# Squares one step later, feed-forward steps dealt by due time, and decay transfers of 104 rows, in a fused RWKV-7 and squared-ReLU kernel

## The chip, the core and the metric

The kernel runs on one core of a Trainium2 chip. Its engines take their instructions in order, each from its own queue, and wait for one another through semaphores: TensorE (PE in the profile, with its weight loads PEld), VectorE (DVE), ScalarE (ACT), GpSimd (POOL) and SyncE (SP), which here only issues DMAs. The metric is the device time of one execution in microseconds (us), taken as the median over several runs.

## What is computed

An attention block (a recurrence over 768 positions, 4 batches, 8 heads of dimension 40) and then a feed-forward block on its output:

```python
for t in range(S):                       # 768 positions, state is D x D per batch and head
    y[:, :, t] = einsum('bhd,bhde->bhe', r_t, state)
    Sa = einsum('bhde,bhe->bhd', state, a_t)
    state = state * w_t - outer(Sa, b_t) + outer(v_t, k_t)
x = y.transpose(0, 2, 1, 3).reshape(B * S, H * D)      # 3072 x 320
out = (maximum(x @ w_in, 0) ** 2) @ w_out              # w_in 320 x 2048, w_out 2048 x 320
```

## The kernel before, in words

**Attention.** The sequence is cut into six chunks of 128 positions, so with four batches there are 24 blocks, called slots here and counted by `i` in `order`. For each slot there are three generators. `early(i)` (L338) turns the decays and the inputs a and b, makes running products of the decays (two scans per pair of heads, L348 and L349, and two reciprocals, L352 and L353), multiplies them into a and b (L356, L357), and stores the result, a tile `decay` of 128 partitions by 1,560 floats, in the DRAM tile `kept_e` (L359). Two heads lie in one tile at partitions 0 and 64, each 40 rows high, so rows 0 to 103 hold data and the rest is padding. `rest(i)` (L491) prepares what can be made before the state is known: it turns k (L501), multiplies it by the decays to `kvT` (L503), multiplies that with a in TensorE (`masked("A", ...)`, L509), turns r and v (L513, L515), makes `RV` (L525), and scales k and b (L535). `chain(i)` (L558) does what needs the state, in up to eleven steps: the products with the state, the solve with two half inverses (`times_t`, L587), the new state (L617), `RX` (L621), and the output `tokens` (L636). `solve` (L411) makes the inverses on GpSimd.

**Decays.** For slots 0 and 1 `early` writes the decays straight into a tile `dec`, taken from a pool of two buffers (L341). From slot 2 on, `load(i)` (L148) takes a `dec` from the same two buffers and loads it from `kept_e`. There are 22 stores and 22 loads, all from SP's queue.

**Feed-forward.** Three slots make a group of 384 tokens (`GB = 3`). When the last slot of a group has its `tokens`, eight small DMAs (L641) move parts of them to other partitions, and two ticks later the group counts as gathered (L642). The generator `ffn()` (L648) then works through the group in 28 steps. Sixteen steps go up: matmuls with `w_third` (for two steps at a time) and `w_in` into PSUM, then a ReLU on ScalarE (L663), then the square of the same tile on VectorE (L664). Twelve steps go down: four matmuls with `w_out` each; every fourth copies its result (L677) and stores 128 tokens (L679). Eight groups are 224 steps in all. A step that is asked for while no group is gathered does nothing (`yield False`).

**The order of the work** is written out by the program itself: the loop at L786 runs `weave` (L691) once per slot, with twelve places per slot. In each place the generators are advanced in a fixed order: `chain(i)`, then the feed-forward, then `early` of a later slot, then `rest(i + 1)`. Each spreads its steps evenly: ten feed-forward steps over twelve places leave places 0 and 6 without one. All engines' queues follow this order. `share` (L782) gives no feed-forward steps to slots 0 to 3, eight to slot 4, and ten to each slot from 5 on; what is left runs after the loop (L812).

The line numbers of the profile are those of the code below.

Of the kernel before, what the change touches and what calls it, by code (L numbers as in the profile page):

```python
# [8 lines left out]
FP32 = mybir.dt.float32  # L9
I32 = mybir.dt.int32  # L10
U32 = mybir.dt.uint32
Alu = mybir.AluOpType
# [5 lines left out]
def kernel(  # L18
# [22 lines left out]
    nc = tc.nc  # L41
    ctx.enter_context(tc.manual_schedule())
    B, H, S, D = r.shape
    DM = H * D
    DFF = moe_w_in.shape[1]
    C = 128
# [3 lines left out]
    NP = H // 2  # L50
    DP = 64
    NF = DFF // 128
    GB = 3
# [7 lines left out]
    for h, d, n in ((6, 0, D), (7, 0, D), (5, HALF, D - HALF)):  # L61
        while n:
# [5 lines left out]
            d, n = d + m_, n - m_  # L68
# [8 lines left out]
    dram = ctx.enter_context(tc.tile_pool(name="dram", bufs=1, space=bass.MemoryType.DRAM))  # L77
# [4 lines left out]
    def psum(pool):  # L82
        name = "ps_" + pool.name[-1]
        return pool.tile([128, 512], FP32, tag=name, name=name)
# [4 lines left out]
    def single(name, shape):  # L89
        return const.tile(shape, FP32, tag=name, name=name)  # L90

    def new(name, shape, bufs):
        return work.tile(shape, FP32, tag=name, name=name, bufs=bufs)
# [4 lines left out]
    def later(fn, steps=2):  # L98
        line.append([steps, fn])
# [7 lines left out]
    def store(out_, in_, steps=2, queue=nc.sync):  # L107
        later(lambda: queue.dma_start(out=out_, in_=in_), steps)  # L108
# [27 lines left out]
    order = [(bb, c) for c in range(NCH) for bb in range(B)]  # L136
# [11 lines left out]
    def load(i, g=None):  # L148
        x_ = loaded[i] = {"k": fetch("k", k, i)}
        if g is not None:  # L150
            g["dec"] = new("dec", [128, 3, NP, C + 2], 2)
            nc.sync.dma_start(out=g["dec"], in_=kept_e[i])
        x_["r"] = fetch("r", r, i)
        later(lambda: x_.update(v=fetch("v", v, i), b=fetch("b", b, i)), 2 if g is not None else 0)

# [22 lines left out]

    UP, DOWN, A_ = range(3)
    decays = Ring("decay", 2, [128, 3, NP, C + 2], 1.0, whole)  # L180
    minus_x = Ring("minus_x", 1, [128, H, DP], 0.0, pads)
    states = Ring("state", B, [128, NP, 2, DP], 0.0, whole)

# [92 lines left out]
    def as_they_are():  # L276
# [4 lines left out]
        for f in range(NF):  # L281
# [6 lines left out]

    kept_n = [dram.tile([HC, H, HC], FP32, tag=f"n{i}", name=f"kept_n{i}") for i in range(len(order))]
    Q = HC // 2  # L290
    kept_e = [dram.tile([128, 3, NP, C + 2], FP32, tag=f"e{i}", name=f"kept_e{i}") for i in range(len(order))]

    sizes = [1, 1] + [2] * 4 + [4] * ((len(order) - 12) // 4) + [2]
    units = [(sum(sizes[:u]), n) for u, n in enumerate(sizes)]
# [11 lines left out]
                        tag=f"t{u}", name=f"kept_t{u}") for u, (_, nb) in enumerate(units)]  # L306
# [31 lines left out]
    def early(i, g=None):  # L338

        x_ = early_loaded.pop(i)  # L340
        dec = decays.next() if g is None else new("dec", [128, 3, NP, C + 2], 2)  # L341
        if g is not None:
            nc.vector.memset(dec[:, :A_, :, MID:MID + 1], 1.0)
        up, down, aT = (dec[:, n] for n in (UP, DOWN, A_))
        wT = turn(x_["w"])
        yield
        for q in range(NP):
            nc.vector.tensor_tensor_scan(up[:, q, MID + 1:C + 1], wT[:, q, MID:], ones, 1.0, Alu.mult, Alu.mult)  # L348
            nc.vector.tensor_tensor_scan(down[:, q, MID - 1::-1], wT[:, q, MID - 1::-1], ones, 1.0, Alu.mult, Alu.mult)  # L349
        yield  # L350
        bT_, aT_ = turn(x_["b"]), turn(x_["a"])
        nc.vector.reciprocal(down[:, :, MID + 1:C + 1], up[:, :, MID + 1:C + 1])  # L352
        nc.vector.reciprocal(up[:, :, :MID], down[:, :, :MID])  # L353
        yield
        bT = turned("bT", 1)
        nc.vector.tensor_tensor(bT, bT_, down[:, :, 1:C + 1], Alu.mult)  # L356
        nc.vector.tensor_tensor(aT[:, :, :C], aT_, up[:, :, :C], Alu.mult)  # L357
        if g is None:
            store(kept_e[i], dec)  # L359
        yield  # L360
        bb, c = order[i]
        t_ = new("N", [128, H, C], 1)
        even, odd = products(bT, aT[:, :, :C])
        nc.scalar.copy(t_[:, :NP], even)

        for half in range(2):
            own_, other = (slice(n * HC, (n + 1) * HC) for n in (half, 1 - half))
            nc.scalar.copy(t_[own_, NP:, own_], odd[other, :, other])
        nc.scalar.copy(t_[:HC, NP:, HC:], odd[:HC, :, HC:])
        joins = lambda half: t_[half * HC:half * HC + Q, :, half * HC + Q:(half + 1) * HC]  # L370
        for half in range(2):
            for n in range(2):
                at = half * HC + n * Q
                if i < SMALL:
                    kept, to = kept_q[i, :, half, n], at + Q
                else:
                    u = unit_of[i]
                    kept, to = kept_d[u][i - units[u][0], :, half], (half + 1) * HC
                    kept = kept[:, n * Q * HC:n * Q * HC + Q * (to - at)].rearrange("h (s t) -> h s t", s=Q)
                store(kept.rearrange("h s t -> s h t"), t_[at:at + Q, :, at:to], 1, nc.scalar if g is not None and n else nc.sync)  # L380
            if i < SMALL and g is None:
                store(kept_m[i][half], joins(half), 1)
        if g is None:
            store(kept_n[i], t_[:HC, :, HC:], 1)
        else:
            g["dec"], g["N"] = dec, new("N21", [HC, H, HC], 2)
            nc.scalar.copy(g["N"], t_[:HC, :, HC:])
            g["joins"] = spare("joins", i)
            for half in range(2):
                nc.scalar.copy(g["joins"][half * HC:half * HC + Q], joins(half))  # L390
        yield
# [253 lines left out]

    PART = NF // 4

    def ffn():  # L648
        for gi in range(len(order) // GB):
            while gi not in gathered or finished[0] < NARROW:  # L650
                yield False
            t_ = tokens.pop(gi)
            hid = []
            for f in range(0, NF, 2):
                ps = [psum(ps_f if gi < len(order) // GB - 1 else ps_w)[:, :GB * C] for _ in range(2)]
                for e, p_ in enumerate(ps):
                    half = slice(e * DP, (e + 1) * DP)
                    mm(p_, w_third[half, f * 64:f * 64 + 128], t_[half, NT, :], True)
                for e, p_ in enumerate(ps):
                    for j in range(NT):  # L660
                        mm(p_, w_in[:, j, (f + e) * 128:(f + e + 1) * 128], t_[:, j, :], False)
                    h_ = hidden[:, f + e]
                    nc.scalar.activation(h_, p_, Act.Relu)  # L663
                    nc.vector.tensor_tensor(h_, h_, h_, Alu.mult)  # L664
                    hid.append(h_)
                    yield True
            while left():
                yield False
            for n in range(GB):
                bb, c = order[gi * GB + n]  # L670
                p_ = psum(ps_f if gi < len(order) // GB - 1 else ps_w)[:, :DM]
                for f in range(NF):
                    mm(p_, hid[f][:, n * C:(n + 1) * C], w_out[:, f], f == 0)
                    if f % PART == PART - 1 and f < NF - 1:
                        yield True
                o_ = new("o", [128, DM], 2)
                nc.scalar.copy(o_, p_)  # L677
                at = bb * S + c * C
                store(out[at:at + C, :], o_)  # L679
                yield True  # L680
# [98 lines left out]
    TOTAL = 12  # L779
    ahead = {0: (4, 5), 1: (6, 7), 2: (8,), 3: (9,), 4: (10, 11), 5: (12, 13)}  # L780
    ahead.update({i: (i + 8,) for i in range(6, len(order) - 8)})
    share = {**{i: (0, 0) for i in range(B)}, B: (8, 4)}  # L782
    pieces_in = {0: (4, TOTAL), 1: (6, TOTAL), 2: (6, TOTAL), 3: (7, TOTAL), B: (4, 4)}
    done = set(range(B))
    unit = unit_of[B]
    for i in range(len(order)):  # L786
        bb, c = order[i]
        n, begin = share.get(i, (10, 0))
        tc.no_sync_barrier()
        g = ready.pop(i)  # L790
        jobs = [(chain(i, g), 11, 0, TOTAL) if i else (first_slot, 10, 0, TOTAL)]
        jobs.append((some(second, n), n, begin, TOTAL))
        made = ahead.get(i, ())
        for j, m_ in enumerate(made):
            jobs.append((prepare(m_), 5, j * 5, TOTAL - 5 * (len(made) - 1 - j)))
        done.update(made)
        if i + 1 < len(order):
            if i:
                ready[i + 1] = {}
                load(i + 1, ready[i + 1])  # L800
            jobs.append((rest(i + 1, ready[i + 1]), 9, 2, TOTAL))
        if i in pieces_in:
            m_, end = pieces_in[i]
            jobs.append((some(rounded, 2 * m_), 2 * m_, 0, end))
        weave(*jobs)
        while unit < len(units) and all(m_ in done for m_ in range(len(order)) if unit_of[m_] == unit):
            flush()
            take(unit, own)
            solve(unit)
            unit += 1  # L810
# [32 lines left out]
```

## Time and profile before

| | |
|---|---|
| median of 6 runs | 1062.65 us (1055.06 to 1066.15) |
| the profiled execution | 1062.29 us, of which the span is 1060.6 us |
| mean granted TensorE clock | 0.903 |
| VectorE, ScalarE, GpSimd busy | 500.1, 272.2, 667.2 us |
| squares L664, 128 of them | 92.7 us, 724 ns each in the mean, 488 to 1623 ns |
| reciprocals L352 | 1740 ns each; scans L348, 267 ns each |
| `kept_e<-decay` and `dec<-kept_e` | 22 each, 780 KB each, issued by SP |
| all DMA traffic | 113.51 MB |
| first feed-forward matmul | 238.6 us |

The span is the time from the first to the last instruction of the execution. "Busy" is the time in which an engine had an instruction in work. The granted clock is the share of full speed that TensorE was given; it changes within a run. In the rows of a window, the columns are: the window, its length, busy time (and number of instructions) of PE, PEld, DVE, ACT and POOL, the granted clock, the DMA engines' mean share, and GB/s. In the rows of a timeline: start, duration, engine, line, operation, output and inputs, form, number of instructions, and in brackets the idle time of the engine before it with what ended it.

### The profile page before, as it was taken

What the parts mean: (1) busy time and instruction counts of PE and PEld (TensorE: products, weight loads), DVE (VectorE), ACT (ScalarE), POOL (GpSimd) and SP (SyncE); (2) the same over time, 40 slices, a digit from 0 to 9 for tenths busy, and PEclk for the clock granted to TensorE, in tenths of its full rate; (3) what the DMA queues carried; (4) which work ended last, traced back from release to release, by engine and by line L of the source; (5) the groups of instructions that cost most, each with busy time, mean ns of one, the idle gap of its engine ahead of it and who ended that gap; (6) DMA issues with size and microseconds to landing.
All of it is one profiled execution on the core that took longest, in us unless ns stands there. A gap on an engine that the chain in (4) does not pass through costs nothing.

```text
span 1060.6 us, 19794 instructions
## 1 busy us (share of the span) xinstructions
PE 942.7 (89%) x7824; PEld 680.5 (64%) x7824; DVE 500.1 (47%) x940; ACT 272.2 (26%) x627; POOL 667.2 (63%) x1124
## 2 busy tenths in 40 slices
PE   6374658769999999999999999999999999999898
PEld 5264556656667766776677667766776577667556
DVE  5465786786463465543662564274324322331120
ACT  3132332442322223113312322123212211231120
POOL 4788465885887699971999943999958960000000
PEclk8666566578889999999999999999999999999899
DMA  8978988857728627348627519504354342220000
GB/s 109 163 141 162 190 223 156 193 132 158 135 60 172 160 25 147 90 89 184 133 33 151 120 72 182 129 34 87 62 136 82 61 97 70 57 37 7 22 1 19
DMA packets 261356, 113.51 MB, mean 107 GB/s; under 512 B 243792, under 2 KB 249424, under 8 KB 259600
## 3 DMA queue, kind: packets, MB, share of 16 engines
q1 hardware_dynamic: 256928, 93.24, 44.5%
q0 software_dynamic: 3248, 18.88, 7.4%
q8 instruction: 62, 1.02, 0.4%
q10 hardware_dynamic: 1088, 0.13, 0.1%
q14 instruction: 30, 0.25, 0.1%
HBM read 75.77 MB, written 34.48 MB: 104 GB/s over the span
## 4 chain that ended last, share of the span: by engine, by line
PE 75%; DVE 7%; DMA 7%; issue 3%; ACT 3%; POOL 3%; SPq 2%; DVEq 0%; ACTq 0%; POOLq 0%
PE ps_f L87 38%; PE ps_c L87 15%; PE ps_w L87 15%; PE ps_w L311 4%; DMA dec<-kept_e 2%; DMA w_out<-in_moe_w_in_dram 1%; SPq L108 1%; POOL half_t L434 1%; POOL half_p L432 1%; DVE decay L352 1%; PE ps_c L577 1%; DMA kept_e<-decay 1%; DVE kvT L503 1%; PE ps_c L541 1%; PE ps_w L531 1%
## 5 line engine op out<-in xcount | busy, mean ns | idle before, releaser
L432 POOL TENSOR_TENSOR half_p<-half_n,half_t 128x70 f32<-128x70 f32 (+52 forms) x502 | 297.5, 593 | 101.2 <-DMA half_n<-kept_d 51.1
L434 POOL TENSOR_TENSOR half_t<-half_t,half_p 128x70 f32<-128x70 f32 (+52 forms) x502 | 322.3, 642 | 39.3
L664 DVE TENSOR_TENSOR hid<-hid 128x384 f32<-128x384 f32 x128 | 92.7, 724 | 245.4 <-ACT hid L663 244.9
L87 PE MATMUL ps_f<-w_out,hid 128*128 128x320 f32 x672 | 200.4, 441 | 0.0
L87 PE MATMUL ps_f<-tokens,w_in 128*128 128x384 f32 x448 | 180.5, 527 | 0.0
L87 PEld LDWEIGHTS ps_f<-w_out,hid 128*128 128x128 f32 x672 | 120.9, 190 | 45.6 <-issue 2.9
L663 ACT ACTIVATE hid<-ps_f 128x384 f32<-128x384 f32 x112 | 54.9, 490 | 265.9 <-PE ps_f L87 265.9
L87 PEld LDWEIGHTS ps_f<-tokens,w_in 128*128 128x128 f32 x448 | 78.9, 196 | 66.3 <-issue 36.3
L87 PE MATMUL ps_f<-tokens,w_third 64*128 64x384 f32 x224 | 55.5, 537 | 2.8 <-DVE w_out L261 2.8
L87 PE MATMUL ps_w<-decay,bT 40*128 40x128 f32 x352 | 29.9, 316 | 30.1 <-DVE decay L357 30.1
L327 DVE TENSOR_TENSOR A<-ps_w,upper 128x512 f32<-128x512 f32 x48 | 30.9, 685 | 45.3 <-PE ps_w L87 45.3
L87 PEld LDWEIGHTS ps_w<-decay,bT 40*128 40x128 f32 x352 | 25.3, 216 | 39.0 <-DVE decay L357 22.6
L348 DVE TENSOR_TENSOR_SCAN decay<-ps_w,ones 128x64 f32<-128x64 f32 x88 | 23.5, 267 | 51.4 <-PE ps_w L311 51.3
L327 DVE TENSOR_TENSOR RX<-ps_w,upper 128x512 f32<-128x512 f32 x48 | 30.8, 683 | 34.3 <-PE ps_w L87 34.1
L87 PE MATMUL ps_w<-dec,kvT 40*128 40x128 f32 x384 | 32.1, 312 | 16.5 <-DVE kvT L503 16.5
L503 DVE TENSOR_TENSOR kvT<-ps_w,dec 128x512 f32<-128x512 f32 x24 | 16.4, 684 | 54.9 <-PE ps_w L311 37.4
L87 PEld LDWEIGHTS ps_w<-dec,kvT 40*128 40x128 f32 x384 | 27.1, 212 | 21.8 <-DVE kvT L503 19.3
L327 DVE TENSOR_TENSOR RV<-ps_w,upper 128x512 f32<-128x512 f32 x48 | 30.9, 685 | 16.3 <-PE ps_w L87 15.8
L352 DVE RECIPROCAL decay<-decay 128x256 f32<-128x256 f32 x22 | 38.3, 1740 | 0.0
L87 PEld LDWEIGHTS ps_c<-xr,T 64*64 64x64 f32 x768 | 29.1, 146 | 14.0 <-issue 10.4
L87 PEld LDWEIGHTS ps_w<-rT,kvT 40*128 40x128 f32 x384 | 27.7, 204 | 15.9 <-DVE RX L327 7.4
L87 PE MATMUL ps_w<-rT,xnT 40*128 40x128 f32 x384 | 34.4, 289 | 3.5 <-ACT rT L513 2.6
(139 smaller groups left out, 1422.2 us busy)
## 6 DMA issues: line engine op xcount, KB each, us to landing
kept_e<-decay SPq DMA_DIRECT2D x22, 780.0 KB
dec<-kept_e SPq DMA_DIRECT2D x22, 780.0 KB
hid<-in_moe_w_out_dram SPq DMA_DIRECT2D x16, 320.0 KB
half_n<-kept_d POOLq DMA_DIRECT2D x12, 384.0 KB, 8.6
half_n<-kept_d POOLq DMA_DIRECT2D x6, 768.0 KB, 10.4
in_w<-in_w_dram SPq DMA_DIRECT2D x24, 160.0 KB
in_ab<-in_b_dram SPq DMA_DIRECT2D x24, 160.0 KB
in_ab<-in_a_dram SPq DMA_DIRECT2D x24, 160.0 KB
```

The costliest lines, as they stand in the source:

```text
L87: nc.tensor.matmul(o, l_, r_, start=start, stop=True, skip_group_check=True)
L108: later(lambda: queue.dma_start(out=out_, in_=in_), steps)
L311: nc.tensor.transpose(p_[:, q * 128:(q + 1) * 128], pair(x_, q), ident)
L327: nc.vector.tensor_tensor(t_, p_, over4(upper), Alu.mult)
L348: nc.vector.tensor_tensor_scan(up[:, q, MID + 1:C + 1], wT[:, q, MID:], ones, 1.0, Alu.mult, Alu.mult)
L352: nc.vector.reciprocal(down[:, :, MID + 1:C + 1], up[:, :, MID + 1:C + 1])
L432: nc.gpsimd.tensor_tensor(p_, part[:, at:at + m_].unsqueeze(1).to_broadcast([128, n, m_]), t3[:, :n, s:s + 1].to_broadcast([128, n, m_]), ...
L434: nc.gpsimd.tensor_tensor(t3[:, :n, s + 1:], t3[:, :n, s + 1:], p_, Alu.subtract)
L503: nc.vector.tensor_tensor(kT, kT_, down[:, :, 1:C + 1], Alu.mult)
L531: nc.tensor.transpose(p_[:, q * 128:(q + 1) * 128], down[:, q, 1:C + 1], ident)
L663: nc.scalar.activation(h_, p_, Act.Relu)
L664: nc.vector.tensor_tensor(h_, h_, h_, Alu.mult)
```

## The change

There are three parts. In the feed-forward, the square of a tile is issued in the following step, after that step's ReLU; the last one is issued at the beginning of the first step down. The steps are dealt by a list `by_then` of how many are to be issued by the end of each slot: at most ten more than the slot before, and from slot 9 on no more than leaves `LAG = 4` of a group for after the slot in which the next group is gathered. The decays' DRAM tiles have 104 rows (`USED = DP + D`), the transfers move these rows only, and the two `dec` buffers are named tiles, `kept_here`, in place of tiles of the pool.

```diff
@@ def load
-            g["dec"] = new("dec", [128, 3, NP, C + 2], 2)
-            nc.sync.dma_start(out=g["dec"], in_=kept_e[i])
+            g["dec"] = kept_here[i % 2]
+            nc.sync.dma_start(out=g["dec"][:USED], in_=kept_e[i])
@@ beside the rings
+    USED = DP + D
+    kept_here = [single(f"dec{n}", [128, 3, NP, C + 2]) for n in range(2)]
@@
-    kept_e = [dram.tile([128, 3, NP, C + 2], FP32, tag=f"e{i}", name=f"kept_e{i}") for i in range(len(order))]
+    kept_e = [dram.tile([USED, 3, NP, C + 2], FP32, tag=f"e{i}", name=f"kept_e{i}") for i in range(len(order))]
@@ def early
-        dec = decays.next() if g is None else new("dec", [128, 3, NP, C + 2], 2)
+        dec = decays.next() if g is None else kept_here[i]
...
-            store(kept_e[i], dec)
+            store(kept_e[i], dec[:USED])
@@ def ffn
+    square = lambda h_: nc.vector.tensor_tensor(h_, h_, h_, Alu.mult)
...
                     nc.scalar.activation(h_, p_, Act.Relu)
-                    nc.vector.tensor_tensor(h_, h_, h_, Alu.mult)
+                    if hid:
+                        square(hid[-1])
                     hid.append(h_)
                     yield True
+            square(hid[-1])
             while left():
@@ before the loop over slots
-    share = {**{i: (0, 0) for i in range(B)}, B: (8, 4)}
+    PER, LAG = NF + 4 * GB, 4
+    by_then = [0] * B + [8]
+    for i in range(B + 1, len(order)):
+        by_then.append(min(by_then[-1] + 10, PER * (i + 1) // GB - PER - LAG if i > 2 * B else PER * i))
+    share = {i: (n - (by_then[i - 1] if i else 0), 4 if i == B else 0) for i, n in enumerate(by_then)}
...
-        n, begin = share.get(i, (10, 0))
+        n, begin = share[i]
```

## The prediction

> **What bounds the kernel now.** I read the table of stages first: each engine's busy time in four stretches, cut where the first feed-forward matmul starts (238.6 us), where the first slots with feed-forward work end, and where the last slot ends.
>
> ```profile
> 0.00:238.00 238.00, 150.13 (x1524) 128.23 (x1524) 162.04 (x332) 79.51 (x182) 167.32 (x437) 0.66 0.85 163
> 238.00:320.00 82.00, 76.95 (x641) 54.58 (x642) 46.86 (x88) 22.34 (x52) 64.53 (x118) 0.86 0.58 116
> 320.00:980.00 660.00, 641.72 (x5359) 453.16 (x5358) 280.31 (x502) 159.19 (x370) 435.34 (x571) 0.99 0.46 97
> 980.00:1061.00 81.00, 73.90 (x303) 44.48 (x301) 10.90 (x19) 11.13 (x24) 0.00 (x0) 0.95 0.04 14
> ```
>
> To 238 us no engine is full: the stage is a chain of transfers and small operations (DMA share 0.85, clock 0.66). From there on TensorE sets the time. The change leaves its matmuls as they are, so it can win only TensorE's idle time, 5.1 + 18.3 + 7.1 = 30.5 us after 238 us, and time at a lowered clock. Who makes TensorE wait between 320 and 980 us, the list of waits names in two lines:
>
> ```profile
> PE ps_w L87 <- DVE kvT L503: 15.5, 10, 2.0
> PE ps_w L87 <- ACT rT L513: 2.4, 10, 0.2
> ```
>
> So 15.5 of 18.3 us are ten waits for `kvT`. The timeline of one of them shows why:
>
> ```profile
> 415.82 0.60 PE L311 MATMUL ps_w<-ident,in_k 128*128 128x128 f32 x4
> ...
> 417.79 1.56 PE L87 MATMUL ps_f<-tokens,w_in 128*128 128x384 f32 x4
> ...
> 419.38 0.49 ACT L663 ACTIVATE hid<-ps_f 128x384 f32<-128x384 f32 x1 [1.74 <-PE ps_f L87]
> ...
> 419.90 0.56 DVE L664 TENSOR_TENSOR hid<-hid 128x384 f32<-128x384 f32 x1 [0.76 <-ACT hid L663]
> 420.38 0.68 DVE L503 TENSOR_TENSOR kvT<-ps_w,dec 128x512 f32<-128x512 f32 x1
> ...
> 421.12 1.16 PE L87 MATMUL ps_w<-dec,kvT 40*128 40x128 f32 x16 [1.33 <-DVE kvT L503]
> ```
>
> The turned k is ready at 416.4, but `kvT` stands behind a square, which waits for the ReLU of a matmul issued later than the turn. TensorE gets through the matmuls between (there is no feed-forward step in place 6) and waits. The same wait costs a second time through the clock. Rows of 2 us after two waits, and the last wait of the span:
>
> ```profile
> 298.00:300.00 2.00, 2.00 (x20) 1.71 (x20) 0.72 (x2) 0.66 (x2) 1.79 (x3) 0.68 0.69 284
> 737.00:739.00 2.00, 2.00 (x5) 0.98 (x5) 0.55 (x1) 0.12 (x1) 1.84 (x3) 0.50 0.03 8
> 998.30 2.99 PE L87 MATMUL ps_w<-tokens,w_third 64*128 64x384 f32 x4 [2.70 <-DMA tokens<-tokens]
> 1001.00:1003.00 2.00, 2.00 (x4) 1.17 (x4) 0.00 (x0) 0.00 (x0) 0.00 (x0) 0.50 0.00 0
> ```
>
> After four of the ten `kvT` waits (382, 733, 842, 915 us) the granted clock is 0.5 for about 3.4 us, which loses half of it, 1.7 us each time. After the wait for L357 at 297.9 us (2.46 us) it stays low to 309 us. After the wait for the last `tokens` DMAs it is low from 998 to 1005 us.
>
> **The squares.** Nothing is added or removed: 128 squares of 0.49 to 1.62 us move one step down VectorE's queue. The square that now stands before `kvT` belongs to the step before; its ReLU is done before the turn of k. At 417 us I lay the rows out again: square to 416.2, eight scans (0.18 us apart) to 417.7, square to 418.3, `kvT` to 419.0, before the transposes of `xn` end at 419.8. **No wait is left: -15.5 us**, and with the waits go their four half-clock stretches, 4 x 1.7 = **-6.8 us**.
>
> Here a rule and the rows part. The Trainium skill ("TensorE: Matmul & The Clock Gate", Part 1: The HAM clock gate) says that the clock is halved after an idle window of about 3.4 us and comes back after a busy one. The length fits the stretches of 3.4 us, but waits of 1.3 to 1.9 us are too short to halve it by that rule, and six waits of the same size were followed by none. By the rule the stretches would have another cause and might stay; by the rows each follows a wait within 3 us. I take the rows, since I found no half-clock stretch after 320 us without such a wait ahead of it.
>
> In slot 5 the wait at 297.9 us is of the same kind. VectorE runs scans (to 288.6), square (waits, 289.3), square (waits, 291.4), two reciprocals (1.74 + 1.69), square (1.08), then L356 and L357 at 0.60 each, with which TensorE was waiting. With the squares ready at once the reciprocals start at 290.2 rather than 291.9, L357 ends near 295.9 and TensorE is free at 295.5: the wait falls from 2.46 to about 0.5 us. With a similar 0.5 us of the 0.74 at 271.8: **-2.5 us**. The low clock from 298 to 309 us lost (0.32 + 0.5 x 4 + 0.24) x 2 = 5.1 us: **-5.1 us**. A third low stretch, 275 to 281 us (3.4 us lost), follows a wait for ACT L478, which the change doesn't touch; I leave it.
>
> What is late next: the copy of r (0.24 us, ten times; stays), then the masks, with 2 us of slack or more. The last square of a group now comes in the first step down; its tile is read by the 16th matmul, three steps of 2.35 us later. The bound from the other side: if another VectorE operation takes the place of `kvT`, the wait could come back whole, 0 of the 15.5.
>
> **The steps dealt anew.** Before, 8 + 19 x 10 = 198 steps are asked for by the end of slot 23, and only 7 x 28 = 196 exist: two are asked in vain, and at the last `tokens` two steps (16 rows, 4.57 us) stand between TensorE and DMAs that take until 998.2. Now the list gives 8, 18, 28, ... 108 to slot 14 as before, then 9, 9, 10 in turn, 192 by the end. So up to slot 14 TensorE's order is the same; after it six slots (15, 16, 18, 19, 21, 22) have nine steps, with none in places 0, 4 and 8. At the end 8 steps down, 8 x 2.33 = 18.6 us, cover the 7.1 us from L636 (991.15) to the DMAs' landing. **The wait of 2.7 us goes, and with it the half clock from 998 to 1005 us, 3.4 us: -6.1 us.**
>
> Cost of the nine-step slots: in place 4, the second `times_t` needs the copies L599 and L600, ready 0.7 us after the matmuls with N (455.12 to 455.82 in the rows of that slot); the turn of k takes 0.5 to 0.6 of it. In place 8, `RX` is ready 1.4 us after its matmuls and is read after the products for `RV`, those with `sd` and those with `RV`, 1.1 us each: no wait. Place 6 has a step now. I put **+1.0 us** for all six; from both sides 0 to 6 x 1.0, the whole of two copies and their starts. The output stores of the moved steps (160 KB each) stand later in SP's queue, behind loads of k, dec and r in slots 20 to 23; those loads then wait for less. The last of them still follows the last copy at 1057.35.
>
> **104 rows.** 44 transfers shrink from 780 to 633.75 KB. Only those in the first 238 us can matter (eight stores and four loads, SP's rows); afterwards no wait of TensorE names them. Three are on the chain of waits there:
>
> ```profile
> 99.73 9.23 DMA kept_e<-decay
> 109.88 9.45 DMA dec<-kept_e
> ...
> 154.13 9.84 DMA dec<-kept_e
> ```
>
> If time goes with bytes, 18.75% of 28.5 = -5.3 us. The Trainium skill ("DMA: Bandwidth & Descriptors", Why a DMA increments its semaphore by 16 and not by 1) says that a transfer is split over the largest number of engines up to 16 that divides the outermost size: 16 for 128 rows, 13 for 104. Either way a busy engine moves 8 rows of 6,240 bytes, and three engines merely stand idle: 0 us. The trace shows no single DMA engine and no transfer of 104 rows; I take **0**, since the share of 0.85 says that engines, not bytes (163 GB/s, against 327 in the best 2 us I saw), fill this stage; -5.3 is kept for the range. The named `dec` tiles leave the loads where they were on SP, behind the same waits.
>
> **Sum.** -15.5 - 6.8 - 2.5 - 5.1 - 6.1 + 1.0 = -35.0 us. The profiled execution took 1062.29, so 1027.3; the median lies 0.4 above it: **1028 us**.
>
> **Rivals.**
> 1. The waits go and the clock stays (0.15): -15.5 - 2.5 - 2.7 + 1.0 = -19.7, **1043 us**. For it: the rule, and six waits without a drop. Against it: the drops' places.
> 2. Time goes with bytes in the first stage (0.12): 5.3 less, **1022 us**.
> 3. Another wait takes the place of `kvT` (0.08): half of the loop's 22.3 us stays, **1039 us**. For it: VectorE's squares and reciprocals last up to 1.7 us each beside GpSimd. Against it: VectorE is 42% busy there.
> 4. Slower: fewer engines carry the 104 rows (0.08). If eight did, each would move 13 rows in place of 8 and a transfer of 9.5 us would take 15.4. Three of them on the chain cost 18 us; it decides from six transfers on (6 x 5.9 = 35); with nine of the twelve, +53 - 35, **1081 us**. Against it: the rule's 13.
>
> **Numbers.** My own case has 0.57. The range 1018 to 1044 takes in rivals 1 to 3 and the stretch at 275 us (3.4). No change means within 0.5% (5.3 us), about what a measurement of this kernel can tell. Faster 0.89, same 0.04, slower 0.07: rival 4 makes the slower and, with just six transfers, 0.01 of the same; the other 0.03 is rival 3 with the whole wait back.
>
> **What would show it.** The line of waits for `kvT` gone between 320 and 980 us, and TensorE busy 99% there; no 0.5 clock after 300 us; the wait of VectorE for L663 down from 245 us to a few tens; the last `tokens` DMAs without a wait; the first `ps_f` matmul still at 238 us, which rival 2 puts earlier and rival 4 later. I am wrong if TensorE waits elsewhere for as long.

## The result, and the profile after

The changed kernel takes 1055.55 us (median of 34 runs, 1050.17 to 1063.13), the kernel before 1060.45 us in the runs made beside it (71 runs). The ratio is **0.9956, with a 95% interval of 0.9943 to 0.9969**: 4.7 us faster, where 35 us were forecast. The profiled executions have spans of 1055.5 and 1060.6 us.

Line numbers below are those of each kernel itself. In the changed kernel the square is L651, the ReLU L668, `kvT` L506, the loads of `T` L451 and the store of the inverses L440; in the kernels of the experiments they differ by a few lines.

The table of stages of the changed kernel, cut as before (window, length, busy time and number of instructions of PE, PEld, DVE, ACT and POOL, granted clock, DMA share, GB/s):

```profile
0.00:238.00 238.00, 163.95 (x1508) 140.74 (x1508) 158.72 (x318) 77.86 (x176) 164.02 (x430) 0.63 0.84 152
238.00:320.00 82.00, 76.99 (x680) 54.96 (x682) 53.14 (x108) 24.89 (x59) 62.23 (x116) 0.92 0.70 121
320.00:980.00 660.00, 641.99 (x5387) 455.17 (x5383) 277.61 (x498) 159.81 (x372) 441.97 (x579) 0.98 0.49 91
980.00:1056.00 76.00, 72.24 (x256) 44.14 (x256) 9.62 (x17) 9.96 (x21) 0.00 (x0) 0.99 0.04 14
```

Two things stand out against the rows of before. In the third row TensorE is busy for 641.99 us where it was 641.72: the idle time between 320 and 980 us is 18.0 us where it was 18.3. And in the first row bytes went down (GB/s from 163 to 152) while the DMA engines' share hardly moved (0.85 to 0.84). The list of TensorE's waits from 320 to 1000 us says what fills the idle time now (who waits, for what, us in total, times, longest):

```profile
PE ps_c L87 <- DMA T<-kept_t: 9.8, 2, 5.4
PE ps_w L314 <- DMA in_r<-in_r_dram: 3.8, 2, 2.8
```

The line for `kvT`, 15.5 us before, is gone. In its place stands `T`, the inverses, for which TensorE did not wait between 320 and 1000 us before.

What the change was to do in a place of the loop, it does. The timeline of the changed kernel around one turn of k:

```profile
408.55 0.60 PE L314 MATMUL ps_w<-ident,in_k 128*128 128x128 f32 x4
...
410.01 1.31 DVE L651 TENSOR_TENSOR hid<-hid 128x384 f32<-128x384 f32 x1
411.25 0.68 DVE L506 TENSOR_TENSOR kvT<-ps_w,dec 128x512 f32<-128x512 f32 x1
412.11 0.49 ACT L668 ACTIVATE hid<-ps_f 128x384 f32<-128x384 f32 x1 [1.74 <-PE ps_f L87]
...
412.44 1.16 PE L87 MATMUL ps_w<-dec,kvT 40*128 40x128 f32 x16
```

The square ahead of `kvT` has no idle time before it, since its ReLU was done long ago. The ReLU of the running step ends at 412.6 us, and `kvT` no longer waits for it. The matmuls with `kvT` start with no idle time of TensorE.

What is late instead, first in the kernel before, then in the changed one (GpSimd's store of the inverses, SP's loads of them, TensorE's first use of them):

```profile
473.13 0.60 POOL L437 DMA_DIRECT2D kept_t<-half_t  x1 [0.30 <-POOL half_t L434]
479.62 2.16 SPq L448 DMA_DIRECT2D T<-kept_t  x2
490.42 0.66 PE L87 MATMUL ps_c<-xr,T 64*64 64x40 f32 x16
```

```profile
478.59 0.60 POOL L440 DMA_DIRECT2D kept_t<-half_t  x1 [0.30 <-POOL half_t L437]
482.80 1.35 SPq L451 DMA_DIRECT2D T<-kept_t  x2
486.54 1.08 PE L87 MATMUL ps_c<-xr,T 64*64 64x40 f32 x16 [5.38 <-DMA T<-kept_t]
505.06 1.05 PE L314 MATMUL ps_w<-ident,in_r 128*128 128x128 f32 x4 [2.84 <-DMA in_r<-in_r_dram]
```

Before, SP issued the loads of `T` at 479.62 and TensorE came to them at 490.42, without a wait. After, TensorE was ready at 481.2, some nine microseconds earlier, while GpSimd stored the inverses 5.5 us later. So it waits 5.38 us. SP's queue is in order, and its own list of waits has one line for these loads:

```profile
SPq L451 <- DMA kept_t<-half_t: 12.5, 1, 12.5
```

For 12.5 us it stands at the loads of `T` until the store has landed. The loads of k, dec and r behind them come out only after that (487.7, 488.3 and 489.0 us), no earlier than before (487.6, 488.2 and 488.9). That r is what TensorE waits for at 505; before, it came to its r at the same time, 505.05 us, and did not wait.

The wait can be worked out. In the changed kernel 4.2 us go by from the store to the loads of `T`, and 3.7 more to the first use. With these times, the kernel before had a slack of 490.42 - 473.13 - 4.2 - 3.7 = 9.4 us. A gain of 9.3 us and a store 5.5 us later leave 9.3 + 5.5 - 9.4 = 5.4 us to wait. In the slots up to 466 us the changed kernel had gained 9.3 us on the kernel before; in this one slot it lost 13.9 (from the times of `tokens` in the two traces).

The second wait for `T`, 4.42 us up to 801.18 us, has another cause. Again the kernel before first (SP's moves of `tokens` at the end of the group), then the changed one:

```profile
783.73 6.85 SPq L108 DMA_DIRECT2D tokens<-tokens  x8
```

```profile
783.00 14.69 SPq L108 DMA_DIRECT2D tokens<-tokens  x8
783.01 0.60 POOL L440 DMA_DIRECT2D kept_t<-half_t  x1 [0.30 <-POOL half_t L437]
783.76 1.95 POOL L412 DMA_DIRECT2D half_n<-kept_d  x4 [0.16 <-issue]
788.50 0.96 POOL L425 MEMSET half_t<- 128x1024 f32 x1 [2.79 <-DMA kept_t<-half_t]
797.78 1.37 SPq L451 DMA_DIRECT2D T<-kept_t  x2
```

These inverses had been stored by 788.5 us, when GpSimd could clear `half_t`. But SP came to the loads of `T` only at 797.78. It stood at the moves of `tokens`, which took 14.69 us where they took 6.85: at the same moment GpSimd stored its inverses and fetched the inputs of its next solve.

The clock, in windows of the changed kernel (the granted clock is the third number from the end):

```profile
298.00:309.00 11.00, 11.00 (x122) 8.26 (x120) 7.71 (x22) 4.43 (x10) 9.93 (x14) 1.00 0.49 108
...
506.00:508.00 2.00, 1.89 (x9) 1.23 (x8) 0.00 (x0) 1.17 (x2) 1.69 (x5) 0.50 1.44 136
```

The low clock from 298 to 309 us is gone with the wait ahead of it, and so is the one after 998 us. But half clock stands from 484 to 491 us, from within the first wait for `T` on, from 505 to 516 us, after the wait for r, and twice later (706 to 714, 802 to 806). Summed over windows of 4 us from 320 to 1000 us, the lowered clock takes 13.7 us in the changed kernel (12.4 without what falls into the waits themselves) and 7.6 before.

### The profile page after: what moved, and what is told of

Same layout as the page of the kernel before. It is cut to its first block, busy times and chain, and to the rows that moved or that the text cites. A ratio compares the mean times of both kernels' runs of the same rounds, so it can differ in the third digit from the quotient of the medians.

```text
span 1055.5 us, 19799 instructions
## 1 busy us (share of the span) xinstructions
PE 955.2 (90%) x7824; PEld 695.0 (66%) x7824; DVE 499.1 (47%) x940; ACT 272.5 (26%) x627; POOL 668.2 (63%) x1124
## 4 chain that ended last, share of the span: by engine, by line
PE 53%; POOL 21%; DMA 13%; issue 4%; DVE 4%; SPq 4%; ACT 2%; POOLq 0%; ACTq 0%; DVEq 0%
PE ps_f L87 24%; PE ps_w L87 12%; PE ps_c L87 12%; POOL half_t L437 10%; POOL half_p L435 9%; PE ps_w L314 3%; DMA half_n<-kept_d 2%; SPq L108 2%; DMA in_v<-in_v_dram 2%; DMA dec<-kept_e 2%; DMA in_r<-in_r_dram 2%; DMA kept_t<-half_t 1%; DMA in_w<-in_w_dram 1%; DMA tokens<-tokens 1%; SPq L142 1%
## 5 line engine op out<-in xcount | busy, mean ns | idle before, releaser
L651 DVE TENSOR_TENSOR hid<-hid 128x384 f32<-128x384 f32 x128 | 92.1, 721 | 179.4 <-ACT hid L668 179.2
L87 PE MATMUL ps_f<-tokens,w_in 128*128 128x384 f32 x448 | 175.8, 516 | 0.0
L668 ACT ACTIVATE hid<-ps_f 128x384 f32<-128x384 f32 x112 | 55.0, 491 | 255.0 <-PE ps_f L87 255.0
L87 PE MATMUL ps_f<-tokens,w_third 64*128 64x384 f32 x224 | 58.1, 548 | 2.8 <-DVE w_out L264 2.8
L506 DVE TENSOR_TENSOR kvT<-ps_w,dec 128x512 f32<-128x512 f32 x24 | 16.5, 687 | 77.9 <-PE ps_w L314 38.7
L87 PE MATMUL ps_c<-xr,T 64*64 64x40 f32 x768 | 37.2, 243 | 11.3 <-DMA T<-kept_t 9.8
L87 PEld LDWEIGHTS ps_w<-decay,bT 40*128 40x128 f32 x352 | 25.6, 218 | 28.8 <-DVE decay L360 13.9
L87 PE MATMUL ps_w<-rT,xnT 40*128 40x128 f32 x384 | 38.2, 313 | 3.1 <-ACT rT L516 1.9
L87 PE MATMUL ps_w<-rT,kvT 40*128 40x128 f32 x384 | 35.1, 325 | 4.1 <-DVE RX L330 3.4
L87 PEld LDWEIGHTS ps_w<-rT,kvT 40*128 40x128 f32 x384 | 30.3, 226 | 12.7 <-DVE RX L330 4.6
```

The source lines that it names most:

```text
L87: nc.tensor.matmul(o, l_, r_, start=start, stop=True, skip_group_check=True)
L506: nc.vector.tensor_tensor(kT, kT_, down[:, :, 1:C + 1], Alu.mult)
L651: square = lambda h_: nc.vector.tensor_tensor(h_, h_, h_, Alu.mult)
```

## The experiments

**The parts one by one.** Four kernels, run beside one another and beside the kernel before (1061.18 us).

Only the rows and the named tiles:

```diff
+    USED = DP + D
-            nc.sync.dma_start(out=g["dec"], in_=kept_e[i])
+            nc.sync.dma_start(out=g["dec"][:USED], in_=kept_e[i])
-            store(kept_e[i], dec)
+            store(kept_e[i], dec[:USED])
```

> The 104-row transfers and the named tiles alone; squares and dealing as before. Theory A (the smaller transfers run on fewer DMA engines and cost time in the first stage): 3 to 6 us slower than before, ratio 1.003 to 1.006, first ps_f matmul at about 243 us as in the changed kernel against 238.6. Theory B (the transfers are neutral, the later start of the changed kernel was chance, and only the wait for the inverses took the gain): ratio 1.000, first ps_f matmul at 238 to 239 us.

1071.46 us, **1.0105 (1.0061 to 1.015)**: rows and named tiles together cost about 11 us. The first feed-forward matmul comes at 244.15 us, against 238.6.

Only the squares:

```diff
-                    nc.vector.tensor_tensor(h_, h_, h_, Alu.mult)
+                    if hid:
+                        square(hid[-1])
...
+            square(hid[-1])
```

> The squares one step later, alone. Both theories: the waits of TensorE for kvT between 320 and 980 us go (15.5 us before), and waits for T<-kept_t or for loads behind it on SP's queue appear. Theory A: ratio 0.990 to 0.994, since the first stage is not delayed and GpSimd's solves start some 5 us earlier than in the changed kernel. Theory B: 0.996 to 0.998. If the inverses were not the bound, my own sum says 0.972.

1045.07 us, **0.984 (0.9805 to 0.9876)**, 17 us faster. The first two lines of its list of waits of TensorE, 320 to 1000 us:

```profile
PE ps_c L87 <- DMA T<-kept_t: 7.7, 2, 4.4
PE ps_w L87 <- DMA tokens<-tokens: 3.2, 2, 2.7
```

So the waits for `T` appear with the squares alone and 128 rows: they do not need the transfers of 104 rows. The first of them, 4.4 us, comes out of the sum made above: 14.3 us gained up to slot 9, a store 0.5 us earlier, 9.4 us of slack. (With the 104 rows alone, and with the dealing alone, there is one wait for `T`, of 1.7 and 2.5 us, of the second kind, behind moves of `tokens` that took 11.3 and 12.7 us.) The wait for `tokens` at the end stays, as it belongs to the dealing.

Only the dealing:

```diff
-        n, begin = share.get(i, (10, 0))
+        n, begin = share[i]
```

> The feed-forward steps dealt anew, alone. Both theories: the wait for the last tokens DMAs (2.7 us) and the half clock behind it go, -6 us, ratio 0.994 to 0.996; the kvT waits stay at about 15 us. If the nine-step slots cost more than thought, 0.997 to 1.000.

1048.4 us, **0.9882 (0.9847 to 0.9916)**, 12.5 us faster. The first line of the same list:

```profile
PE ps_w L87 <- DVE kvT L503: 6.7, 6, 1.7
```

The dealing takes away the wait for `tokens` and also four of the ten waits for `kvT`, since it moves squares as well. It also adds one: in the first slot with nine steps, slot 15, TensorE waits 1.77 us for `RX`, with half clock behind it. The lowered clock between 320 and 1000 us costs only 3.4 us here. The wait for the decays at 298 us stays (L357, 2.4 us).

Squares and dealing together, with 128 rows:

> Squares later and steps dealt anew, with the decays' transfers of 128 rows and pool tiles as before: the change without its third part. Theory A: faster than the changed kernel (0.9956) by the 3 to 6 us of the first stage, ratio 0.990 to 0.992. Theory B: the same as the changed kernel, 0.995 to 0.997.

1043.08 us, **0.9833 (0.9799 to 0.9868)**. The two parts gave 17.0 and 12.5 us alone and give 17.7 together. TensorE waits 8.5 us for `T` in this kernel, and the first of the two waits, 6.2 us up to 481.8, stands where the changed kernel has it (14.8 us gained, a store 0.8 us later, less 9.4). This kernel beats both the kernel before and the changed one. All four ratios lie outside what I had expected: each part does more, for good or ill, than either theory gave it.

**Is it 104 rows, or the named tiles?** The same edit as in the first experiment with another number, and the whole change with it:

```diff
-    USED = DP + D
+    USED = 112
```

> As the 104-row kernel (named tiles, squares and dealing as before), with 112 rows in place of 104: 112 is 16 x 7, 104 is 13 x 8. Theory A (a transfer is split evenly over the largest number of engines that divides the rows, and the 104 rows cost because three engines stand idle and the other thirteen take everything): 112 rows go over 16 engines, 7 rows each in place of 8, ratio 0.995 to 1.000, no loss. Theory C (the named tiles, or transfers of part of a tile, cost the 10 us): ratio about 1.010, as with 104 rows.

> All three parts of the change, with 112 rows in place of 104. Theory A: as squares and dealing with 128 rows (0.983) or a little faster, 0.979 to 0.984. Theory C: as the changed kernel, 0.995.

Alone: 1059.46 us, **1.0022 (0.9994 to 1.005)**, no difference that can be told. The whole change with 112 rows: 1044.89 us, **0.988 (0.9855 to 0.9904)**. The named tiles do not explain the 11 us: they are in both kernels, and only the number of rows differs. Both ratios lie a little above what I had expected for 112 rows. The intervals of 0.988 and of 0.9833, with 128 rows and pool tiles, overlap, so a few microseconds for 112 rows or for the named tiles are not excluded. In the first stage of the changed kernel and of the kernel with squares, dealing and 128 rows the cost of 104 can be seen growing. SP's loads of `dec`, first of the changed kernel, then of the other:

```profile
155.46 0.54 SPq L152 DMA_DIRECT2D dec<-kept_e  x1
...
234.05 0.55 SPq L152 DMA_DIRECT2D dec<-kept_e  x1
```

```profile
153.54 0.57 SPq L152 DMA_DIRECT2D dec<-kept_e  x1
...
226.69 0.63 SPq L152 DMA_DIRECT2D dec<-kept_e  x1
```

The lag is 1.9 us at the second load and 7.4 us at the fourth. The first feed-forward matmul comes at 243.15 us against 237.42. By the times of `tokens` the gap is 5.5 us up to slot 9, at 466 us, and grows to 11.5 us from slot 10 to slot 18, with longer stretches of half clock and a longer second wait for `T`. So only half of the loss arises in the first 238 us. Whether the other half comes from the later start or from the later transfers, no run tells.

**The transfers by themselves.** Two kernels only store a tile of 6,240 bytes a row to DRAM and load it back, first one at a time, then six stores and six loads in flight.

```python
kinds = (("full", 128), ("fifteen", 120), ("thirteen", 104), ("four", 64))
nc.sync.dma_start(out=kept[nm][0], in_=here[nm][0][:rows])
nc.sync.dma_start(out=here[nm][0][:rows], in_=kept[nm][0])
```

> Only transfers, nothing of the reference is computed and the output is zeros: stores and loads of 128, 112, 104 and 96 rows of 6,240 bytes, first one at a time, each waiting for the one before, then six stores followed by six loads in flight together. Theory A: one at a time, 104 rows take as long as 128, and 112 and 96 take less (7 and 6 rows per engine in place of 8); in flight, 104 takes as long as 128, 112 is 12% and 96 is 25% shorter in the part that scales. If time goes with bytes: 104 rows lie between 96 and 112. If 104 rows go over eight engines: 1.6 times as long as 128.

> Leaves out the whole computation: only transfers, as in the measurement before, with tiles of 128, 120, 104 and 64 rows of 6,240 bytes. 128 rows took 7.7 us for one store and the load after it, 104 rows 9.9. If a transfer on fewer than 16 engines costs more in itself, 120 rows (15 engines with eight rows each) take 9 us or more as well. If it is something of 104 rows or of 13 engines alone, 120 rows take 7.7 +- 0.4. 64 rows (16 engines with four rows each) tell whether bytes count at all: below 6.5 us if they do, near 7.7 if a fixed part rules.

The timeline of the second, at the stores; a store is issued when the load before it has landed, so the distance of two stores is one store and one load, one at a time:

```profile
45.54 0.32 SPq L61 DMA_DIRECT2D kept_full<-full  x1
...
53.15 0.32 SPq L61 DMA_DIRECT2D kept_full<-full  x1
...
69.56 0.32 SPq L61 DMA_DIRECT2D kept_fifteen<-fifteen  x1
...
79.76 0.32 SPq L61 DMA_DIRECT2D kept_fifteen<-fifteen  x1
```

| rows | engines by the rule of the prediction | one store and load, us | six and six in flight, first store to last landing, us |
|---|---|---|---|
| 128 | 16 | 7.6, 7.7 | 25.3 to 27.7 |
| 120 | 15 | 10.1, 10.2 | 34.5, 34.8 |
| 112 | 16 | 8.0 to 8.2 | 31.1, 31.2 |
| 104 | 13 | 9.9 to 10.2 | 29.6 to 30.0 |
| 96 | 16 | 7.6 to 7.9 | 29.7, 30.0 |
| 64 | 16 | 7.4 | 25.1 |

112 and 96 are from the first of the two kernels, 120 and 64 from the second, 128 and 104 from both; each kernel was run once. One at a time, the two sizes that sixteen does not divide stand apart: about 10 us against 7.4 to 8.2. That is none of the three outcomes expected of the first kernel, and what the second was expected to show if fewer engines cost by themselves. Bytes hardly count there, since 64 rows take 7.4 us and 128 take 7.7. In flight no smaller tile beats 128 rows by more than 128 rows differ among themselves, and 104 rows take 2 to 5 us more. But 112 and 96 rows take as long as 104 or longer: six at a time, the sizes that sixteen divides do not stand apart. It is the measurement one at a time that goes with what the kernel does.

That 104 rows do go over 13 engines is seen in the profile's packet counts. The kernel before has 261,356 packets, the changed one 260,168. The 1,188 fewer are 27 in each of 44 transfers: 24 rows and three engines, if each engine adds one packet of its own. The kernel with 112 rows has 704 fewer, 16 in each: 16 rows and no engine. The two kernels of transfers alone, with 23,496 and 22,496 packets in SP's queue, come out to the packet with the engines of the table and one more for each row.

**Are the inverses what holds the rest?** In the kernel with both parts and 128 rows, every second step of the elimination in the longer solves (64 columns) is left out, so that GpSimd is busy about half as long:

```diff
+            if not fine and s % 2:
+                continue
```

> Squares and dealing with 128-row transfers, and every second elimination step of the 64-wide solves on GpSimd left out, so that GpSimd has about half the work there. Theory A (with the kvT waits gone the inverses bound the slots): the waits for T<-kept_t and for loads behind it on SP's queue vanish, and the half clock behind them; the time comes near the sum of the prediction, ratio 0.967 to 0.975. Rival D (something in TensorE's own order or in the first stage takes the rest): 0.981 to 0.984, as with the whole solves.

1031.55 us, **0.9749 (0.9725 to 0.9774)**, against 0.9833. No wait for `T` is left; two lines of what remains between 320 and 1000 us:

```profile
PE ps_w L311 <- DMA in_r<-in_r_dram: 1.8, 1, 1.8
PE ps_w L87 <- DVE RX L327: 0.6, 1, 0.6
```

TensorE is busy for 654.26 of the 660 us to 980 us. Against the kernel with the whole solves, 11.6 us are won in slot 10, where the first wait for `T` stood. The moves of `tokens` at 769 us take 6.34 us here, since GpSimd's fetch no longer falls together with them. VectorE's busy time falls too, from 491.8 to 477.3 us, so a GpSimd that disturbs VectorE less is a rival. In both kernels TensorE waits for VectorE only 0.6 us, for `RX`, between 320 and 1000 us, which leaves that rival little room. To separate the two, the next kernel keeps all the work and changes only the order of the solves:

```diff
-    sizes = [1, 1] + [2] * 4 + [4] * ((len(order) - 12) // 4) + [2]
+    sizes = [1, 1] + [2] * 5 + [4] * ((len(order) - 12) // 4)
```

> Squares later and steps dealt anew, decays of 128 rows, and the inverses' units cut as 1, 1, five times 2, three times 4 in place of 1, 1, four times 2, three times 4 and a 2: the same number of units and the same work, but the inverses of slots 10 and 11 are ready after a pair's solve (about 90 us from 344 us, so near 432) rather than after a four's at 474 us. If TensorE's two waits for T (8.5 us without this) come from the order of GpSimd's solves, both lines are gone, the half clock after them too, and the ratio is 0.972 to 0.978, as where half of the solves' steps were left out (0.9749). If those 0.9749 came from a GpSimd that disturbs VectorE less, the ratio stays at 0.982 to 0.985 though the waits for T are gone. If T's way through SP's queue is what is late, the waits stay, and the ratio is 0.983.

1066.96 us, **1.0093 (1.0064 to 1.0123)**: a miss in its size and its sign. The first wait went, as expected: slots 10 and 11 have their inverses at 431 us. But slots 12 to 15 now hang on one solve of four, which begins after that. The timeline of this kernel:

```profile
565.68 0.60 POOL L437 DMA_DIRECT2D kept_t<-half_t  x1 [0.30 <-POOL half_t L434]
573.30 1.08 PE L87 MATMUL ps_c<-xr,T 64*64 64x40 f32 x16 [23.88 <-DMA T<-kept_t]
```

Slot 12 needs them at 549 us, where this wait begins; the order I chose was wrong for it. The miss is a measurement all the same. The waits for `T` are 33.6 us here against 8.5 us without this edit, 25.1 more, and the ratio is 0.026 higher, which is 27.5 us of 1057.55. No other wait in the list grew by more than 0.3 us. So the time of this kernel follows the waits for the inverses nearly one to one. The solves run back to back from 152 us to 566 us, but for some 12 us at each start, in which the next inputs are fetched, so this order won one wait and made a longer one. It does not settle the rival of VectorE, which stays open as far as the 0.6 us leave room for it.

## Why the prediction was wrong

The direction was right, but the forecast of 1028 us was too low by 27.5 us, and 4.7 us lie within the 5.3 us that the prediction itself called no change and gave 0.04. In the measured ratios, the way from the 35.0 us forecast to the 4.7 us measured has three pieces, each a difference of measured ratios and, by their intervals, uncertain by 3 to 5 us: 104 rows, 0.9956 - 0.9833, **+13.0 us**; the inverses and what comes with GpSimd's solves, 0.9833 - 0.9749, **+8.9 us**; and what even the kernel with the shortened solves did not reach, 35.0 - 26.6 = **+8.4 us**.

- **"104 rows ... I take 0"** is the step that failed most. The count of engines was right. What failed was the inference from it: that 13 engines with eight rows each take as long as 16 with eight rows each. They take 2.2 to 2.6 us more for a store and a load, one after the other, and in the kernel 11 to 13 us in all. About half of it appears after 466 us, where the prediction allowed none ("Only those in the first 238 us can matter"). The bounds were drawn at -5.3 and 0, with a cost only in a rival that supposed another number of engines; nothing in the trace of before excluded a cost with 13. That rival (1081 us) named the right part with the wrong mechanism. The Trainium skill ("DMA: Bandwidth & Descriptors", Why a DMA increments its semaphore by 16 and not by 1) gives the split, which the packets confirm, but not what a split over fewer engines costs in time.
- **"What is late next: ... then the masks, with 2 us of slack or more"** is the second. I looked for the next wait only on VectorE, in the places of `kvT`. The next one came through GpSimd, the store and SP's queue: the loads of `T` were issued at 479.62 and used at 490.42, and once the time gained up to that slot had used the slack up, TensorE met it. The second wait came through the moves of `tokens` in the same queue, slowed beside GpSimd's fetch; no step of the prediction had such a meeting of transfers. A rival had another wait in the place of `kvT`, at 0.08 and with the wrong engine.
- **-15.5 for the ten waits for `kvT`** holds as far as the line goes: it is gone. As time it was not won in full, since the idle time from 320 to 980 us is 18.0 us where it was 18.3.
- **-6.8 for four half-clock stretches** failed with it. They followed waits, as I had read, so with new waits came new stretches: 13.7 us lost in place of 7.6. Even in the kernel with half the steps of the solves, 8.5 us are lost (685 to 693 us after a wait of 0.58 us for `RX`, 722 to 734 us after one of 1.80 us for r). That is as much as the third piece; the forecast had left nothing of it, since the 0.8 of the 7.6 beyond the 6.8 belong to the stretch at 998 us, which it counted elsewhere.
- **+1.0 for the six nine-step slots** was too small. "In place 8 ... no wait" fails in slot 15: the products for `RV` wait there for the VectorE operation that makes `RX`, 1.06 us in the changed kernel and 0.58 to 1.77 us in the others with the new dealing, and half clock follows, from 706 to 714 us in the changed kernel, 3.3 us lost.
- **-2.5 and -5.1 around the wait for L357** hold: the wait is in none of the kernels with the squares moved, and it is in those without (before, rows alone with 104 or 112, dealing alone), and the clock from 298 to 309 us is 1.00.
- **-6.1 at the end** holds: the wait for the last `tokens` is gone and the clock from 998 to 1005 us is 1.00. But the dealing alone gave 12.5 us, more than the 5.1 of its step, since it takes four of the waits for `kvT` too. The parts were no sum: each removes waits that the other removes as well, and together they run into the same waits for `T`.
- **The sign to look for, "the wait of VectorE for L663 down ... to a few tens"**, was a bad one. It fell from 244.9 to 179.2 us. VectorE is busy for 277.61 of 660 us and so reaches its next square early wherever that stands; such a wait costs something only where TensorE waits for what comes behind it, as for `kvT` and for L357.
- **The clock's rule against the rows.** The Trainium skill ("TensorE: Matmul & The Clock Gate", Part 1: The HAM clock gate) has the clock halve after an idle window of about 3.4 us. The rows won for the stretches at 298 and 998 us, which went with their waits of 2.5 and 2.7 us, shorter than that. In the long waits the rule fits: in the first wait for `T` half clock begins 3.5 us after the start of the wait (at 484.64 us, worked out from the clock of 0.82 between 484 and 485 us). That a wait of 0.58 us is enough by itself is not shown.

## What to carry to other kernels

Before a wait is costed as gain, measure the slack of every other input of the same and of the next slots, down each queue: the distance from the issue of its load to its first use, against all the time that the change wins up to that slot. Look also at which transfers will now fall together. An engine that is 67% busy over the stage, as GpSimd is, can be the next bound when its work comes in blocks that are used whole. And a transfer need not be cheaper for having fewer rows: here the numbers of rows that sixteen does not divide were the slow ones one at a time, so measure a new number before using it.

## What was not expected of the hardware

A store and a load of 104 or 120 rows took 9.9 to 10.2 us one at a time, those of 64, 96, 112 and 128 rows 7.4 to 8.2 us. With six in flight, loads of 128 rows landed 1.9 us apart, and those of 112 and 96 rows mostly 2.4 to 2.6 us apart though they are smaller. For 120 rows it was 3.1 to 3.3 us for most. Why fewer engines cost time per transfer, and why 112 and 96 rows are no faster in flight than 128, no run here tells.

The eight moves of `tokens` took SP 6.3 to 6.9 us in nearly all groups of all kernels, and 11.3 to 14.7 us in the six kernels in which GpSimd had stored its inverses and begun to fetch its next inputs up to 4 us before.

Half clock came after shorter waits than I had looked for, down to one of 0.58 us, and not after all of them (not after a wait of 2.02 us for `kvT` at 695 us in the kernel before); what else it needs is open.
